# A hand-written list of 888 steps, put in another order: loads, matrix products and vector work of an RWKV layer with a feed-forward stage

## The chip, the cores and the metric

The kernel runs on one core of a Trainium2 chip. The metric is the device time of one execution in microseconds (us). Five engines work at once, each through its own queue of instructions in order: PE (the matrix engine, with its weight loads shown apart as PEld), DVE (the vector engine), ACT (activations), POOL (GpSimd) and SP (it only issues transfers here). Semaphores tie the queues together.

## The reference

Two stages follow each other: an RWKV attention over 4 batches, 8 heads, 768 positions and 48 values a head, and a feed-forward stage on its 3072 rows of 384 values.

```python
    for t in range(S):
        kt, vt, rt = (k[:, :, t].copy(), v[:, :, t].copy(), r[:, :, t].copy())
        cur = np.einsum('bhd,bhe->bhde', u[None] * kt, vt)
        y[:, :, t] = np.einsum('bhd,bhde->bhe', rt, state + cur)
        state = w[None, :, :, None] * state + np.einsum('bhd,bhe->bhde', kt, vt)
...
    h = x @ w_in                      # 384 -> 2048
    g = np.maximum(0.01 * h, h)
    return (g @ w_out).astype(np.float32)   # 2048 -> 384
```

## The kernel before

The positions are cut into 24 tiles of 128 (n = 0 to 23, six to a batch); a state of 8 heads x 48 x 48 is carried from tile to tile within a batch. The feed-forward stage takes two tiles at a time (m = 0 to 11).

The whole program is a list of steps, `ORDER`. A loop at the end of the kernel goes through it, and each step adds one instruction, or one group of matmuls, to the queue of its engine. So the list alone sets the order on every engine; waits are worked out afterwards from what each step reads and writes. Buffers are rings (`RINGS`): 10 slots for k and r, 10 for v, 6 for the masked scores `at`, 3 for `gT`. A number behind `@` in a step's name is the PSUM bank it takes; the next step on that bank waits until the last reader has let it go.

The steps are named by a letter and their tile. Those that the text speaks of, with their lines in the profile of before:

- `k3`, `r3`, `v3` (L284, POOL): the load of a tile of k, r or v from DRAM, cast to bf16. `i0` to `i3` (L296): a quarter of w_in. `w0` to `w3` (L300): a quarter of w_out. `p1` (L306): u. `p9` (L348, POOL): the ramp from which mask and tables are made.
- `P` (L399, DVE): k and r times their tables. `T` (L421, PE): transposes for tiles 0 to 7, which ACT copies out (`C`, L432). From tile 8 on `X` (L410, SP) transposes by DMA.
- `A` (L481, PE): scores; `M` (L491, L502, L505, DVE): scores under the mask, into `at`. For tiles 6 and up `E`, `f`, `R` (L442, L447, L452, DVE) make a token's own weight, and `L` (L467, POOL) lays it on the diagonal of `at` before `M` runs.
- `K` (L535, L539, L544, PE): keys times values; `V` (L560, DVE): v scaled, for tiles 0 to 5; `B` and `W` (L570 or L573, and L578, DVE): the next state. `Y` (L609, L613, PE): outputs of a tile; `O` (L627, ACT): copied to `xT`.
- `G` (L642, PE): 12 matmuls of 128 columns, the first product of the feed-forward stage for one tile, used for tiles 0 and 1; `J` (L664, PE): 6 matmuls of 256 columns, the same for two tiles; `j` (L673, ACT): the leaky relu.
- `b` (L735, DVE) and `t` (L716, DVE): sums for a seven-product form of the second matrix product; `Z` (L766, PE): one of the seven, 8 matmuls of 192 columns; `z` (L777, L782 on ACT, L787, L792 on DVE): its result; `o` (SP): the store.
- `F` (L387, PE): a matmul on a tile of ones whose result is not used.

```python
    for name in ORDER.split():
        unit[0] = name
        steps[name[0]](*(int(x) for x in name[1:].split("@")[0].split(".") if x))
```

Of the kernel before, what the change touches and what calls it, by code (L numbers as in the profile page):

```python
# [11 lines left out]
B, H, S, D = 4, 8, 768, 48  # L12
L = 128
# [4 lines left out]
E = 64  # L18
# [25 lines left out]
f7 J1.5@0 R6 O5 R7 j1.1 K6@7 L6 A7@23 B6 j1.5 A6@45 J2.6@6 j1.4 L7 M6 J2.1@7 k10 J0.5@0 M7 j2.1 J2.4@1 k11 j0.5
b1.0 Y6@7 j2.4 r10 Y7@0 b0.0 J2.5@5 O7 v8 b0.1 O6 J2.7@4 j2.6 b1.1 r11 J2.3@7 j2.7 J2.0@6 j2.5 k13 t0 j2.3
J2.2@0 j2.0 Z0.0@7 b1.2 j2.2 P9 Z0.1@1 z0.0 t1 X9 Z1.0@0 b2.0 J3.1@2 b0.3 Z0.2 P8 Z1.1@3 z0.2 z1.0 t2 X8 z0.1
Z0.3@4 j3.1 J3.3@5 E9 E8 Z0.4 k18 P10 j3.3 f8 K7@6 z1.1 Z1.2 t3 X10 k12 J3.2@2 z1.2 B7 r12 Z1.3@5 f9 E10 r15
z0.4 Z0.5 W7 P11 J3.6@6 r18 f10 X11 z0.5 Z0.6 b1.3 v16 Z1.4 R8 j3.6 E11 J3.7@1 L8 R9 J3.5@6 z1.3 j3.7 R10 r14
J3.4@5 z0.6 z0.3 j3.2 P13 v12 K8@1 J3.0@7 f11 j3.4 B8 j3.5 L9 A8@45 z1.4 A9@12 M8 Z1.5 k15 Z2.0@6 M9 L10 Z1.6
Y8@4 r16 W8 z1.6 j3.0 z1.5 Y9@5 P12 O8 A10@01 R11 X12 A11@23 O9 Z3.0@7 E12 L11 E13 M10 J4.4@4 X13 J4.3@5 v13  # L50
j4.4 b3.0 J4.7@0 v18 M11 J4.2@1 v14 J4.0@4 b3.1 j4.2 K9@2 j4.3 k14 J4.5@3 P15 z2.0 j4.7 J4.6@1 b3.3 X15 v19 j4.5
B9 Z3.1@5 j4.6 v10 b2.1 Z2.1@0 z3.0 z3.1 b2.2 k16 Z3.2 W9 b2.3 J4.1@3 k17 z3.2 z2.1 f12 Z2.2 f13 j4.1 v11 b3.2
Z2.3@2 z2.2 R12 j4.0 r19 K12@1 Z2.4 B12 L12 Z2.5 z2.3 R13 A12@12 z2.5 L13 A13@34 M12 Z3.3@0 k19 Z3.4 z2.4 P14
Z3.5 k21 z3.4 X14 Z2.6 z3.3 v15 M13 Z4.0@2 r17 K10@1 K13@0 B10 Y12@3 Y13@4 k20 O12 W10 Y10@1 P16 O13 Y11@3 v22
O10 P18 J6.0@4 O11 P19 z2.6 r20 J5.7@1 E16 E14 J5.4@3 E15 r22 j5.7 E17 b4.2 J6.1@6 j5.4 v20 z3.5 J5.6@1 f15 j6.1
f16 r23 J5.5@3 f14 j5.6 b4.0 J5.1@5 z4.0 v21 j5.5 B13 J6.6@6 P17 j5.1 f17 J5.3@3 X17 j6.0 R14 J5.0@5 b4.1 L14
j5.3 R15 J5.2@4 X18 j5.0 E18 Z3.6 r21 j5.2 b4.3 J6.7@3 z3.6 E19 k22 j6.6 W13 J6.5@7 o0 j6.7 X16 L15 A14@01 j6.5
A15@34 M14 J6.4@5 J6.3@6 j6.4 f18 o1 M15 J6.2@7 o7 o4 K14@5 Z4.1@0 o6 P20 Z4.2 B14 z4.1 j6.2 K15@1 W14 Z4.3@3
j6.3 P21 z4.2 R18 Y14@4 X21 f19 Y15@5 L18 O14 R19 A18@67 O15 K16@4 z4.3 Z4.4 P22 J7.7@5 B15 X22 z4.4 J7.3@3 W15
K18@1 Z4.5 X19 B18 Z4.6 B16 R17 J7.6@1 j7.7 M18 L17 X20 J7.4@4 j7.6 J7.5@5 v17 b6.0 j7.4 J7.2@1 j7.3 b5.0 o2 k23  # L60
z4.6 J7.0@4 j7.5 b5.1 v23 j7.2 J7.1@6 z4.5 R16 j7.0 o8 A17@01 W16 o3 j7.1 A16@23 L16 M17 o5 A19@45 Z5.0@7 L19
Z5.1@6 M16 Z6.0@0 E20 Z6.1@1 z6.0 M19 z5.0 K19@2 Z5.2 b6.1 Y18@3 Y19@4 E21 O18 Y17@5 B19 O19 Y16@3 f21 b5.3
J9.3@2 O16 f20 z6.1 Z6.2 O17 b6.2 Z5.3@3 b5.2 j9.3 E22 J8.3@4 R20 J8.0@5 R21 j8.3 L20 P23 J8.1@2 j8.0 L21 J9.2@4
# [12 lines left out]
"""


# [87 lines left out]
def bass_rwkv5_eagle__then__act_leaky_relu_kernel(  # L166
# [16 lines left out]
    NQK, NTP, NVS, NAT, NT, NX, NG, NO, NRK, NV = RINGS  # L183
# [4 lines left out]
    r_sb, k_sb = rk_sb[:, :, 0, :], rk_sb[:, :, 1, :]  # L188
    v_sb = SB("v_sb", [128, NV, H * E])
# [80 lines left out]

    def load_one(which, n):
        b, c = divmod(n, NC)
        t0 = c * L
        src = {"k": k, "r": r, "v": v}[which][b].rearrange("h t d -> t h d")[t0:t0 + L, :, :]
        if which == "v":
            dst = v_sb[:, n % NV, :].rearrange("p (h e) -> p h e", e=E)[:, :, 0:D]
        else:
            dst = {"k": k_sb, "r": r_sb}[which][:, n % NRK, :].rearrange("p (h d) -> p h d", d=D)
        key = (which, n % (NV if which == "v" else NRK))
        if which == "v" and n in VHW:  # L280
            io = 6 + n
            add("sp", lambda: SP.dma_start(hd(out_sb[io][:, :]), src), W=[("o", io, 0), ("o", io, 1)], dma=f"v{n}")
        else:
            add("pool", lambda: G.dma_start(dst, src), W=[key], dma=f"{which}{n}")  # L284
# [585 lines left out]
```

## Time and profile before

| | us |
|---|---|
| three runs | 165.57, 164.47, 164.97 |
| median | 164.97 |
| the profiled execution | 165.07 |
| its span (first to last instruction) | 163.3 |
| PE busy | 154.8 (95%) |
| DVE busy | 130.5 (80%) |
| ACT busy | 88.2 (54%) |
| POOL busy | 88.1 (54%) |

What lies between the span and the execution's time, 1.8 us, is outside the instructions. The busy shares are means over the whole span; the text below reads them stage by stage. A row of a timeline gives the start, the duration, the engine, the line, the operation, its result and operands, how many neighbours were merged into it, and in brackets how long the engine had been idle before it and who ended that. Durations of matmuls overlap, so the distance between two starts is the better measure there.

### The profile page before, as it was taken

What the parts mean: (1) busy time and instruction counts of PE and PEld (TensorE: products, weight loads), DVE (VectorE), ACT (ScalarE), POOL (GpSimd) and SP (SyncE); (2) the same over time, 40 slices, a digit from 0 to 9 for tenths busy, and PEclk for the clock granted to TensorE, in tenths of its full rate; (3) what the DMA queues carried; (4) which work ended last, traced back from release to release, by engine and by line L of the source; (5) the groups of instructions that cost most, each with busy time, mean ns of one, the idle gap of its engine ahead of it and who ended that gap; (6) DMA issues with size and microseconds to landing.
All of it is one profiled execution on the core that took longest, in us unless ns stands there. A gap on an engine that the chain in (4) does not pass through costs nothing.

```text
span 163.3 us, 5367 instructions
## 1 busy us (share of the span) xinstructions
PE 154.8 (95%) x2299; PEld 137.6 (84%) x2299; DVE 130.5 (80%) x260; ACT 88.2 (54%) x194; POOL 88.1 (54%) x101
## 2 busy tenths in 40 slices
PE   5959999999999698999999999999999999999993
PEld 1737888888999587999898998989989999999992
DVE  2678978979989999999999999999867770561552
ACT  3486686979443334722795528359057454637120
POOL 7999999996079958999974229223032000000000
PEclk9999999999999999999999999999999999999999
DMA  6999999999999999999999999900261000005025
GB/s 105 137 167 167 154 174 163 186 204 144 145 121 161 100 151 152 130 145 87 150 131 211 264 128 151 230 4 0 62 199 52 0 4 0 0 18 180 4 98 193
DMA packets 100234, 19.89 MB, mean 122 GB/s; under 512 B 93169, under 2 KB 100210, under 8 KB 100210
## 3 DMA queue, kind: packets, MB, share of 16 engines
q0 software_dynamic: 75616, 10.03, 93.8%
q1 hardware_dynamic: 23266, 9.12, 30.4%
q10 hardware_dynamic: 1328, 0.39, 1.0%
q8 instruction: 18, 0.29, 0.7%
q14 instruction: 6, 0.05, 0.1%
HBM read 20.65 MB, written 4.72 MB: 155 GB/s over the span
## 4 chain that ended last, share of the span: by engine, by line
PE 60%; POOL 21%; DVE 9%; DMA 6%; issue 2%; POOLq 0%; DVEq 0%
PE ps_all L766 28%; PE ps_all L664 25%; POOL rk_sb L284 11%; DMA rk_sb<-in_r_dram 6%; POOL v_sb L284 4%; PE ps_all L609 3%; PE ps_all L481 2%; POOL w_out_sb L300 2%; POOL w_in_sb L296 2%; DVE qk L399 2%; DVE at L505 2%; POOL at L467 1%; PE ps_all L539 1%; DVE out_sb L787 1%; DVE s_tok L452 1%
## 5 line engine op out<-in xcount | busy, mean ns | idle before, releaser
L673 ACT ACTIVATE gT<-ps_all 128x512 bf16<-128x512 f32 x92 | 52.0, 604 | 29.3 <-PE ps_all L766 14.1
L664 PE MATMUL ps_all<-xT,w_in_sb 128*128 128x256 bf16 x552 | 66.6, 273 | 0.5 <-DVE at L505 0.5
L664 PEld LDWEIGHTS ps_all<-xT,w_in_sb 128*128 128x128 bf16 x552 | 52.4, 98 | 7.3 <-DVE at L505 0.8
L467 POOL TENSOR_SCALAR_AFFINE_SELECT at<-s_tok 128x1024 bf16<-128x1024 f32 x18 | 20.6, 1155 | 27.0 <-DVE s_tok L452 26.9
L766 PE MATMUL ps_all<-tw,gs 128*128 128x192 bf16 x288 | 28.3, 246 | 0.1
L735 DVE TENSOR_TENSOR gs<-gT 128x1024 bf16<-128x1024 bf16 x24 | 16.1, 686 | 11.1 <-ACT gT L673 5.8
L284 POOL DMA_DIRECT2D rk_sb<-in_k_dram x23 | 21.0, 918 | 7.2 <-DVE ku L442 6.4
L766 PEld LDWEIGHTS ps_all<-tw,gs 128*128 128x128 bf16 x288 | 24.0, 98 | 0.4 <-issue 0.3
L505 DVE CAST_PREDICATED at<-mask,ps_all 128x1024 bf16<-128x1024 uint16 x18 | 21.5, 1216 | 2.0 <-PE ps_all L481 1.8
L284 POOL DMA_DIRECT2D v_sb<-in_v_dram x23 | 21.1, 923 | 0.6 <-PE ps_all L539 0.6
L284 POOL DMA_DIRECT2D rk_sb<-in_r_dram x23 | 21.3, 932 | 0.0
L766 PE MATMUL ps_all<-w_out_sb,gT 128*128 128x192 bf16 x192 | 19.8, 246 | 0.0
L787 DVE TENSOR_TENSOR out_sb<-ps_all,snap 128x192 f32<-128x192 f32 x37 | 12.6, 351 | 5.9 <-PE ps_all L766 5.8
L627 ACT ACTIVATE xT<-ps_all 128x384 bf16<-128x384 f32 x24 | 11.0, 494 | 11.5 <-PE ps_all L609 10.3
L777 ACT ACTIVATE snap<-ps_all 128x192 f32<-128x192 f32 x36 | 11.1, 338 | 11.3 <-PE ps_all L766 10.3
L766 PEld LDWEIGHTS ps_all<-w_out_sb,gT 128*128 128x128 bf16 x192 | 16.1, 98 | 0.5
L399 DVE TENSOR_TENSOR qk<-rk_sb,tab 128x768 bf16<-128x768 bf16 x23 | 13.9, 611 | 2.9 <-DMA rk_sb<-in_r_dram 2.7
L609 PE MATMUL ps_all<-at,v_sb 128*32 128x128 bf16 x384 | 10.4, 220 | 1.1 <-DVE vs L560 1.1
L432 ACT ACTIVATE tp<-ps_all 128x512 bf16<-128x512 f32 x16 | 9.0, 596 | 3.9 <-PE ps_all L421 3.6
L609 PEld LDWEIGHTS ps_all<-at,v_sb 128*32 128x32 bf16 x384 | 8.0, 96 | 3.1 <-DVE vs L560 1.4
L766 PE MATMUL ps_all<-w_out_sb,gs 128*128 128x192 bf16 x96 | 9.9, 246 | 0.0
L782 ACT ACTIVATE out_sb<-ps_all 128x192 f32<-128x192 f32 x11 | 3.7, 332 | 11.3 <-PE ps_all L766 11.3
(69 smaller groups left out, 196.6 us busy)
## 6 DMA issues: line engine op xcount, KB each, us to landing
out_dram<-out_sb SPq DMA_DIRECT2D x22, 192.0 KB, 2.8
rk_sb<-in_k_dram POOLq DMA_DIRECT2D x23, 96.0 KB, 6.0
rk_sb<-in_r_dram POOLq DMA_DIRECT2D x23, 96.0 KB, 6.0
v_sb<-in_v_dram POOLq DMA_DIRECT2D x23, 96.0 KB, 5.5
w_in_sb<-in_moe_w_in_dram POOLq DMA_DIRECT2D x4, 384.0 KB, 6.4
w_out_sb<-in_moe_w_out_dram POOLq DMA_DIRECT2D x4, 384.0 KB, 11.1
tp<-qk SPq DMA_TRANSPOSE x16, 5.2
out_sb<-in_k_dram ACTq DMA_DIRECT2D x1, 192.0 KB, 2.8
```

What stands on the lines that cost most here:

```text
L284: add("pool", lambda: G.dma_start(dst, src), W=[key], dma=f"{which}{n}")
L399: add("dve", lambda: V.tensor_tensor(qk[iq][:, :, 0:D], both, by, ALU.mult), R=[("r", n % NRK), ("k", n % NRK), "qtab", "ktab", ("qk0", iq ...
L467: add("pool", lambda: G.affine_select(out=at[ia][:, :, :, :].rearrange("p two m i -> p (two m) i"), in_=s_tok[i2][:, :].unsqueeze(2).to_br ...
L505: add("dve", lambda: V.copy_predicated(dst, mask[:, :].bitcast(mybir.dt.uint16).unsqueeze(1).to_broadcast([128, H, 128]), raw), R=keys + [ ...
L609: last = PE.matmul(ps_y[32 * q:32 * q + 32, 128 * s:128 * s + 128], a, m, start=first_mm and (s == 0 or whole), stop=last_mm and whole)
L627: add("act", lambda: A.activation(xT[m % NX][:, :, 128 * half:128 * half + 128], ps[i][:, 0:HD].rearrange("p (s t) -> p s t", t=128), AF.C ...
L664: last = PE.matmul(ps[i][:, 256 * f:256 * f + 256], w_in_sb[:, s, 128 * fb:128 * fb + 128], xT[ix][:, s, :], start=s == 0, stop=s == NSL - 1)
L673: add("act", lambda: A.activation(gT[ig][:, 2 * j:2 * j + 2, :].rearrange("p f t -> p (f t)"), ps[i][:, :], AF.Prelu, alpha=0.01), R=[key] ...
L735: add(eng, lambda: on.tensor_tensor(x[i][:, :, :], a, b, op), R=keys, W=[("gs", m % 2, i)])
L766: done = PE.matmul(ps[i][:, 0:NH], lhs[:, s, :], rhs[:, s, :], start=bool(opens) and s == 0, stop=s == HF - 1, skip_group_check=not (opens ...
L777: add("act", lambda: A.activation(snap[i2][j][:, :], ps[i][:, 0:NH], AF.Copy), R=[key], W=[("snap", i2, j)])
L787: add("dve", lambda: V.tensor_tensor(out_sb[io][:, cols], ps[i][:, 0:NH], snap[i2][j][:, :], ALU.add), R=[key, ("snap", i2, j), *after], W ...
```

## The change

The list is put in another order. No step of the computation is added or taken away; only the unused matmuls `F` become 10 where they were 21. The load function is written so that it could take two tiles at once, but the set that would ask for it, `PAIRED`, is empty, so each load has the same shape as before.

```diff
 VHW = {0}
+PAIRED = set()
...
 ORDER = """
-p3 p0 q1 k1 p10 p2 p8 p11 p4 F1.256.10@0 F1.256.2@1 k2 p5 p21@7 p6 p9 r1 p7 p15 p17 p13 p16 F1.512.18@6 v0 r2
...
+p3 p0 p9 q1 q0 p2 p8 p19 k3 p18 p14 p15 p13 p11 p4 p17 p10 p5 p16 r1 p21@0 p6 k1 p7 v0 p22 k2 p24 p23 r3 P0.1
...
     def load_one(which, n):
         b, c = divmod(n, NC)
-        t0 = c * L
-        src = {"k": k, "r": r, "v": v}[which][b].rearrange("h t d -> t h d")[t0:t0 + L, :, :]
...
+        m, slots = (2 if n in PAIRED else 1), (NV if which == "v" else NRK)
+        i = n % slots
+        src = {"k": k, "r": r, "v": v}[which][b].rearrange("h (c t) d -> t c h d", t=L)[:, c:c + m, :, :]
...
+        if m == 1:
+            src, dst = src[:, 0, :, :], dst[:, 0, :, :]
```

Three places matter for what follows. The lines of the new file stand one lower than those of the old one.

First POOL, from its first load on. Before, these are k1, k2, the ramp, r1, r2, the quarter i1 of w_in, r3, k3, v1, k5, r5, v2, i0:

```order
L284 DMA rk_sb<-in_k_dram 128x8x48 x2
L348 IOTA ramp 128x128
L284 DMA rk_sb<-in_r_dram 128x8x48 x2
L296 DMA w_in_sb<-in_moe_w_in_dram 128x3x512
L284 DMA rk_sb<-in_r_dram 128x8x48
L284 DMA rk_sb<-in_k_dram 128x8x48
L284 DMA v_sb<-in_v_dram 128x8x48
```

Now they are the ramp, k3, r1, k1 and k2, r3, v1, r2, and then i1:

```order
L347 IOTA ramp 128x128
L283 DMA rk_sb<-in_k_dram 128x8x48
L283 DMA rk_sb<-in_r_dram 128x8x48
L283 DMA rk_sb<-in_k_dram 128x8x48 x2
L283 DMA rk_sb<-in_r_dram 128x8x48
L283 DMA v_sb<-in_v_dram 128x8x48
L283 DMA rk_sb<-in_r_dram 128x8x48
L295 DMA w_in_sb<-in_moe_w_in_dram 128x3x512
```

The ramp and three loads of tiles 1 and 3 moved ahead of r2 and of the w_in quarter; after thirteen loads (k5, r5, v2, i0 and v3 follow in both) the same data have been asked for.

Second PE, at K3 (prod3, the matmuls on `wu`, and qk3) and the four G groups. Before: T5, then G1.1 and G1.0, K3, G0.0, and then Y2 begins (G0.1 stands ten steps earlier):

```order
L421 MATMUL ps_all<-ident,qk5 128x128 x8
L642 MATMUL ps_all<-xT0,w_in_sb 128x128 x24
L535 MATMUL ps_all<-wu,prod3 128x2 x4
L539 MATMUL ps_all<-v_sb,qk3 128x96 x4
L642 MATMUL ps_all<-xT0,w_in_sb 128x128 x12
L609 MATMUL ps_all<-at2,v_sb 32x128 x4
```

Now, from the last matmuls of Y2 (vs2) on:

```order
L612 MATMUL ps_all<-ident,vs2 128x128 x3
L641 MATMUL ps_all<-xT0,w_in_sb 128x128 x12
L534 MATMUL ps_all<-wu,prod3 128x2 x4
L538 MATMUL ps_all<-v_sb,qk3 128x96 x4
L641 MATMUL ps_all<-xT0,w_in_sb 128x128 x12
L608 MATMUL ps_all<-at3,v_sb 32x128 x4
```

K3 has moved behind Y2 and behind all G groups but the last.

Third DVE, around B8 (sum_t0), which frees the bank of A9 (before) or A8 (now), and M8 (at2). Before, P13 (qk1) and f11 (ku3) stand ahead of B8:

```order
L787 TENSOR_TENSOR out_sb0<-ps_all,snap0_0 128x192
L399 TENSOR_TENSOR qk1<-rk_sb,tab 128x16x48
L447 TENSOR_TENSOR ku3<-rk_sb,ku3 128x384
L573 TENSOR_TENSOR sum_t0<-ps_all,st2 128x384
L787 TENSOR_TENSOR out_sb3<-ps_all,snap1_1 128x192
L505 COPY_PREDICATED at2<-mask,ps_all 128x1024
```

Now:

```order
L398 TENSOR_TENSOR qk1<-rk_sb,tab 128x16x48
L451 TENSOR_REDUCE s_tok1<-ku1 128x8
L441 TENSOR_TENSOR ku3<-rk_sb,u_tab 128x384
L786 TENSOR_TENSOR out_sb2<-ps_all,snap1_0 128x192
L451 TENSOR_REDUCE s_tok0<-ku0 128x8
L451 TENSOR_REDUCE s_tok2<-ku2 128x8
L786 TENSOR_TENSOR out_sb0<-ps_all,snap0_0 128x192
L572 TENSOR_TENSOR sum_t0<-ps_all,st2 128x384
L446 TENSOR_TENSOR ku3<-rk_sb,ku3 128x384
```

P13 has moved ahead of three sums (R9, R8, R10), and f11 behind B8.

More of the change, by code (lines that the diff above doesn't have):

```diff
@@ L44 @@
[L44 to L63, printed above, removed]
@@ new lines @@
+f17 O14 R18 K16@7 O15 Z4.4 P22 L18 J7.3@3 R17 X22 z4.4 Z4.5 j7.3 L17 M18 J7.7@2 X19 v17 K18@3 Z4.6 W15 z4.5 z4.3
+J7.4@0 B16 o2 J7.5@1 b5.1 X20 j7.4 R19 J7.6@5 j7.7 b6.0 j7.5 L19 J7.0@0 j7.6 b6.2 o3 J7.1@6 z4.6 f16 j7.0 B18
+J7.2@7 j7.1 R16 A17@01 j7.2 W16 A19@23 L16 A16@45 M19 Z5.0@6 k23 Z6.0@7 z5.0 M16 Z6.1@2 r23 Z5.1@3 M17 K19@4
+Z5.2 b6.1 Y18@5 Y19@0 E22 O18 B19 Y16@1 O19 Y17@5 f22 E21 J9.3@4 R22 O17 O16 b5.2 J9.1@0 L22 j9.3 b6.3 J8.0@5
+z6.0 P23 Z5.3@1 j8.0 E20 X23 f21 J8.1@4 z5.2 W19 z5.1 z5.3 Z6.2 E23 j8.1 o8 J9.2@5 o6 f23 o7 b7.0 J8.3@1 j9.2 o9
@@ L283, in load_one @@
         else:
-            add("pool", lambda: G.dma_start(dst, src), W=[key], dma=f"{which}{n}")
+            add("pool", lambda: G.dma_start(dst, src), W=[(which, i + j) for j in range(m)], dma=f"{which}{n}")
     def v_cast(n):
```

62 lines of the change are left out of this document (36 added, 26 removed).

## Prediction

> **What bounds the kernel now.** I read the busy time by stage first, then who waited for whom, then the timelines of PE, DVE and POOL where PE stood still. The columns of the stages are the busy time (and count) of PE, PEld, DVE, ACT and POOL.
>
> ```profile
> 0.00:22.60 22.60, 18.86 (x304) 13.32 (x305) 15.69 (x43) 14.13 (x28) 21.42 (x30) 1.00 1.82 149
> 22.60:62.60 40.00, 38.09 (x570) 33.68 (x568) 37.31 (x69) 23.77 (x50) 31.45 (x36) 1.00 1.99 150
> 62.60:107.60 45.00, 44.98 (x738) 40.94 (x739) 44.21 (x85) 24.90 (x56) 30.67 (x33) 1.00 1.66 159
> 107.60:163.30 55.70, 52.91 (x691) 49.62 (x689) 33.34 (x66) 25.41 (x61) 4.59 (x4) 1.00 0.19 60
> ```
>
> From 22.60 us on PE is idle for 1.91 us in the second stage, 0.02 us in the third and 2.79 us in the last, nearly all of that after its last matmul. So PE sets the pace, and a new order can win in three ways only: the dense part begins earlier, the waits inside it go, or the tail shrinks. DVE is next: 44.21 of 45.00 us in the third stage, with no cover for more work there. The two waits that make up the 1.91 us are these:
>
> ```profile
> PE ps_all L481 <- DVE sum_t L573: 1.4, 1, 1.4
> PE ps_all L664 <- DVE at L505: 0.5, 1, 0.5
> ```
>
> The price of PE's work comes from the chain of waits, where the matmuls stand back to back (start, length, line and count):
>
> ```profile
> 75.68 0.34 PE ps_all L539 x8
> 77.53 7.32 PE ps_all L664 x66
> 148.75 11.89 PE ps_all L766 x144
> ```
>
> A J is 6 x 7.32/66 = 0.67 us, a Z 8 x 11.89/144 = 0.66 us, the usual K 0.17 us. Both lists hold the same J, Z, K, A and Y, so inside the dense part PE needs the same time in both.
>
> **The start.** The first J of before begins at 22.67 us; the set of PE steps that stands ahead of it is the same in the new list, but for the unused F. So the question is when the first J runs now.
>
> ```profile
> 3.61 0.23 DVE L357 TENSOR_SCALAR ident<-ramp 128x128 bf16<-128x128 f32 x1 [1.88 <-POOL ramp L348]
> 8.77 0.56 DVE L399 TENSOR_TENSOR qk<-rk_sb,tab 128x768 bf16<-128x768 bf16 x1 [2.15 <-DMA rk_sb<-in_r_dram]
> 12.04 0.95 POOL L284 DMA_DIRECT2D v_sb<-in_v_dram  x1
> v_sb<-in_v_dram POOLq DMA_DIRECT2D x1, 96.0 KB, 7.1
> 17.84 1.51 PE L642 MATMUL ps_all<-xT,w_in_sb 128*128 128x128 bf16 x24
> 19.29 0.24 PE L535 MATMUL ps_all<-wu,prod 128*128 128x2 bf16 x4
> 19.76 0.55 DVE L560 TENSOR_TENSOR vs<-v_sb,ps_all 128x384 bf16<-128x384 bf16 x1
> 22.67 2.13 PE L664 MATMUL ps_all<-xT,w_in_sb 128*128 128x256 bf16 x18
> ```
>
> The ramp, now first, ends DVE's 1.88 us of idling, but DVE waits next for the third load anyway (r1 before, at 8.77 us; k1 now, also third), so that gains nothing. The thirteenth load, v3, is the thirteenth in both lists: issued at 12.04, landed 7.1 us later at 19.1. K3 followed at 19.29 and V3 at 19.76, so neither the loads nor i1's later place (its G groups all start after 14.7 us, against about 13.4 for the eighth load) move this point. What does is PE's order. Before, K3 runs right after G1.1 and G1.0. Now it stands behind Y2 and G1.0, and Y2 behind V2. From the starts of PE's rows, a G group is 0.76 us (1.51 for two), and from G1.1 on the new list has G1.1, K2, G0.1, T5.1, Y2, G1.0, K3: 0.76 + 0.44 + 0.76 + 0.27 + 0.78 + 0.76 = 3.8 us from G1.1 to K3. G1.1 needs Y1, which I put at about 15.1 us by adding DVE's rows from P1 on, so G1.1 starts near 16.8, K3 near 20.6, V3 at 21.0, Y3 at 21.5 and the first J at 23.4. That is **0.7 us later**. The bounds: 0 if the G groups run while Y1 is awaited elsewhere, 1.5 if the chain slips by one T, C and D more.
>
> **The waits inside.** Here is what PE waited for, and the POOL rows beside it.
>
> ```profile
> L442 DVE TENSOR_TENSOR ku<-rk_sb,u_tab x18: 346/351/1242, 29.5 to 111.0; 128x384 bf16<-128x384 bf16 x18
> L447 DVE TENSOR_TENSOR ku<-rk_sb,ku x18: 345/351/1533, 30.9 to 112.3; 128x384 bf16<-128x384 bf16 x18
> 52.88 1.21 DVE L399 TENSOR_TENSOR qk<-rk_sb,tab 128x768 bf16<-128x768 bf16 x1
> 54.01 1.53 DVE L447 TENSOR_TENSOR ku<-rk_sb,ku 128x384 bf16<-128x384 bf16 x1
> 54.21 1.11 POOL L467 TENSOR_SCALAR_AFFINE_SELECT at<-s_tok 128x1024 bf16<-128x1024 f32 x1
> 55.47 0.54 DVE L573 TENSOR_TENSOR sum_t<-ps_all,st 128x384 bf16<-128x384 f32 x1
> 56.07 0.40 PE L481 MATMUL ps_all<-tp 48*128 48x128 bf16 x8 [1.39 <-DVE sum_t L573]
> 59.92 1.51 DVE L442 TENSOR_TENSOR ku<-rk_sb,u_tab 128x384 bf16<-128x384 bf16 x2
> 60.09 1.14 POOL L467 TENSOR_SCALAR_AFFINE_SELECT at<-s_tok 128x1024 bf16<-128x1024 f32 x1 [1.95 <-DVE s_tok L452]
> 62.62 1.59 PE L664 MATMUL ps_all<-xT,w_in_sb 128*128 128x256 bf16 x13 [0.55 <-DVE at L505]
> ```
>
> A step f has a median of 351 ns; f11 took 1533 and ended 0.2 us after the GpSimd select beside it; E13 likewise ended with the select of 60.09. So a two-input bf16 step on DVE that meets a select loses about 1 us, and B8, queued behind P13 and f11, came late; A9 waited 1.39 us for its bank. In the new list f11 stands behind B8, and between K8 and A8 PE has three more Z and J steps (2.0 us). Adding DVE's rows from P9 on (P9 cannot begin before k9, now the 26th small load):
>
> ```profile
> 30.20 1.02 POOL L284 DMA_DIRECT2D rk_sb<-in_k_dram  x1
> rk_sb<-in_k_dram POOLq DMA_DIRECT2D x1, 96.0 KB, 12.4
> ```
>
> The 26th of before (k8) was issued at 30.20 and landed 12.4 us later, at 42.6. From there DVE's steps to B8 sum to 10.3 us, with one wait of about 0.6 us for K7, which moved later on PE: B8 ends near 54.0, and A8 is due at 54.29 + 0.7 = 55.0. So the 1.39 us goes. M10, which set the 0.55 us, then ends near 60.6 and its J is due at 60.9: cover of only 0.3 us, gone if P12 meets the select L11. I keep half of that wait: the term is **-1.6 us** (bounds -1.94 and 0, the second if the lost time returns as in the row at 54.01). X9 to X11 and their transposes start 2 us later on SP, but A9 takes them ten microseconds afterwards.
>
> **A new wait late on.**
>
> ```profile
> 80.65 0.95 POOL L284 DMA_DIRECT2D rk_sb<-in_r_dram  x1
> 98.95 0.88 POOL L284 DMA_DIRECT2D rk_sb<-in_k_dram  x1
> rk_sb<-in_k_dram POOLq DMA_DIRECT2D x1, 96.0 KB, 5.3
> 100.79 2.19 POOL L467 TENSOR_SCALAR_AFFINE_SELECT at<-s_tok 128x1024 bf16<-128x1024 f32 x2
> 109.64 1.20 DVE L399 TENSOR_TENSOR qk<-rk_sb,tab 128x768 bf16<-128x768 bf16 x1
> ```
>
> r23 was issued at 80.65; now it is queued behind the select L16 and behind k23. L16 waits for R16, at about 101.4 on the old clock; with 1.1 for L16 and 0.9 for k23, r23 goes out at 103.4 and, at 5.3 us like k23, lands at 108.7, at worst at 110. Its reader P23 moves up to 108.6. Behind P23 on DVE stand E20, f21, W19 and z5.3, and J8.3 needs z5.3's bank at 111.3, 0.7 us after z5.3 is due. So P23 may lose 0 to 1.4 us, of which 0.7 is covered: 0 to 0.7 for PE; I take **+0.3**.
>
> The other moves cost nothing: r18 now waits for f8 where k18 waited for E8, both near 45.5 us; ACT is busy 24.90 of 45.00 us, and the stores at the end have the same last one.
>
> **The sum** is 0.7 - 1.6 + 0.3 = -0.6 us, from the profiled execution's 165.07: **164.4 us**, 0.3% under the median of 164.97. About 1% (163.3 to 166.6) is what a measurement of this kernel can tell from no change.
>
> **The rivals.** *All waits go and the start holds*: 165.07 - 1.94 = 163.1. For it: K3 may overlap more than I add; against it: PE's order at K3 in plain sight.
>
> *PE is cold for longer.*
>
> ```profile
> 3.77 2.95 PE L387 MATMUL ps_all<-ones 128*128 128x512 bf16 x13
> 7.80 0.58 PE L421 MATMUL ps_all<-ident,qk 128*128 128x128 bf16 x4
> 9.39 0.40 PE L421 MATMUL ps_all<-ident,qk 128*128 128x128 bf16 x4 [0.79 <-DVE qk L399]
> ```
>
> The same four transposes took 0.58 us at 7.80 and 0.40 at 9.39: PE came to full speed in between, about 6 us after its first matmul, and 13 F in a row filled the time from 3.77. Now 10 F are left, most of them behind steps that wait for data. If PE stays slow until the G groups, the short steps on the way (T, K, Y) cost 1.5 us more and half of the 3.8 us from G1.1 to K3 are spent again at half speed, 1.5: 164.4 + 3.0 = 167.4. Against it: from T1 on PE has work every few tenths of a microsecond in both lists. [...]
>
> *DVE is held by selects in the full stage*, the case on the other side.
>
> ```profile
> 84.25 0.78 DVE L442 TENSOR_TENSOR ku<-rk_sb,u_tab 128x384 bf16<-128x384 bf16 x1
> 85.55 1.24 DVE L442 TENSOR_TENSOR ku<-rk_sb,u_tab 128x384 bf16<-128x384 bf16 x1
> 86.72 1.24 DVE L578 TENSOR_TENSOR st<-sum_t,wl 128x384 bf16<-128x384 bf16 x1
> ```
>
> In the third stage of before three steps met a select and lost 0.43, 0.89 and 0.89 us, 2.2 in all. In the new list a sum R, which lets a select go, is followed at once by two-input steps in five places (R12 by b2.3; R14 by E15 and P19; R15 by b5.0, E18; R19 by b6.0, b6.2; R22 by b5.2, b6.3): 5 x 0.9 = 4.5 us, 2.3 more than before, on an engine with 0.79 us to spare in 45. If all meet, and J4.7's wait of 0.3 returns, the time is 164.4 + 2.3 + 0.3 = 167.0. It decides from the point where DVE's lead on PE, 0 to 1 us here, is used up. Against it: a step that starts before its select loses nothing, as the E of 346 ns, the median, show.
>
> **How the numbers follow.** Forecast 0.48 (its own range 163.4 to 165.7), all waits gone 0.24, cold PE 0.12, DVE held 0.16. Faster by over 1%: the second case and a rest of the first, 0.26; slower: most of the last two, 0.25; within: 0.49. The range goes from just under the second case, 162.7, to the price of the two slow ones, 167.2.
>
> **What would show it.** The first J after 23 us; no wait of PE for sum_t near 55 us; a wait of DVE for in_r_dram near 108 us; PE without idle time between. The forecast is wrong if PE waits over 1 us in any stage after 62 us, if the early transposes take 0.58 us beyond 12 us, or if the first J comes before 22.7.

## The result, and the profile after

The changed kernel takes 166.99 us (median of 6 runs, 166.85 to 167.61), the kernel before 165.27 us (6 runs). The ratio is 1.0111, with a 95% interval of 1.0068 to 1.0154: 1.1% slower, where 0.3% faster was forecast. The profiled execution has a span of 165.2 us, 1.9 us more than before. All ratios here leave out executions over 1.5% above the fastest of their kernel; only in `l10_later` are these many, five of twelve (the median of all twelve is 167.28 us).

First the same four stages as in the prediction (busy time and count of PE, PEld, DVE, ACT, POOL).

```profile
0.00:22.60 22.60, 16.33 (x263) 11.72 (x267) 15.62 (x42) 12.46 (x25) 21.63 (x30) 1.00 1.82 146
22.60:62.60 40.00, 38.60 (x604) 33.72 (x593) 35.58 (x68) 25.37 (x55) 29.75 (x34) 1.00 1.92 155
62.60:107.60 45.00, 44.28 (x683) 39.96 (x685) 43.74 (x82) 23.30 (x51) 31.96 (x34) 1.00 1.52 135
107.60:165.30 57.70, 54.80 (x772) 51.29 (x758) 35.06 (x71) 27.47 (x66) 7.85 (x5) 1.00 0.28 74
```

The first stage has 16.33 us of PE work where before had 18.86; of the 2.53 us between them 1.95 are unused matmuls (5.27 us before, 3.32 now). In the second PE is idle for 1.40 us, in the third for 0.72; before it was 1.91 and 0.02. So the start lost, and the waits inside were not removed but exchanged. What PE waited for, by line:

```profile
PE ps_all L420 <- DVE qk L398: 1.1, 1, 1.1
PE ps_all L608 <- DVE at L504: 0.8, 2, 0.5
PE ps_all L480 <- DVE st L569: 0.7, 1, 0.7
PE ps_all L663 <- issue: 0.6, 1, 0.6
PE ps_all L641 <- issue: 0.6, 1, 0.6
```

The waits for `sum_t` at A9 (1.39 us) and for `at` at J4.7 (0.55 us) are gone, the first as forecast, while the forecast had kept half of the second. New are two waits of Y8 and Y9 for M8 and M9, one of A19 for B18, and two that are put down to "issue": PE waited there for nothing that the profile shows. They stand in the middle of a group, behind the fifth matmul of G1.0 and behind the third of J1.5:

```profile
12.53 0.60 PE L420 MATMUL ps_all<-ident,qk 128*128 128x128 bf16 x4
19.81 0.44 PE L641 MATMUL ps_all<-xT,w_in_sb 128*128 128x128 bf16 x5
20.83 0.56 PE L641 MATMUL ps_all<-xT,w_in_sb 128*128 128x128 bf16 x7 [0.58 <-issue]
23.97 2.13 PE L663 MATMUL ps_all<-xT,w_in_sb 128*128 128x256 bf16 x18
35.63 1.80 PE L663 MATMUL ps_all<-xT,w_in_sb 128*128 128x256 bf16 x15 [0.58 <-issue]
```

The first row is T3.0 at 12.53 us, still 0.6 us long; in before the transposes were at 0.40 from 9.39 us on. The fourth row is the first J with its neighbours, at 23.97 us.

The two waits of Y8 and Y9 have one cause, which DVE's and POOL's timelines show together (W8 is L577, L10 the select at 56.64, M8 and M9 are L504):

```profile
55.72 0.92 POOL L283 DMA_DIRECT2D v_sb<-in_v_dram  x1
55.96 2.02 DVE L577 TENSOR_TENSOR st<-sum_t,wl 128x384 bf16<-128x384 bf16 x1
56.64 1.11 POOL L466 TENSOR_SCALAR_AFFINE_SELECT at<-s_tok 128x1024 bf16<-128x1024 f32 x1
58.16 2.34 DVE L504 CAST_PREDICATED at<-mask,ps_all 128x1024 bf16<-128x1024 uint16 x2
59.52 0.24 PE L608 MATMUL ps_all<-at,v_sb 128*32 128x128 bf16 x4 [0.35 <-DVE at L504]
60.56 0.24 PE L608 MATMUL ps_all<-at,v_sb 128*32 128x128 bf16 x4 [0.47 <-DVE at L504]
```

W8 took 2.02 us instead of 0.35 and ended 0.2 us after the select. The wait of A19 is the same story: one of two b (0.68 us alone) met the select L19, so B18 (L569) came late.

```profile
99.90 2.17 DVE L734 TENSOR_TENSOR gs<-gT 128x1024 bf16<-128x1024 bf16 x2
100.05 1.47 POOL L466 TENSOR_SCALAR_AFFINE_SELECT at<-s_tok 128x1024 bf16<-128x1024 f32 x1 [1.77 <-DVE s_tok L451]
102.26 0.54 DVE L569 TENSOR_TENSOR st<-ps_all,wl 128x384 bf16<-128x384 f32 x1
102.86 0.62 PE L480 MATMUL ps_all<-tp 48*128 48x128 bf16 x16 [0.72 <-DVE st L569]
```

### The profile page after: what moved, and what is told of

Its sections match the earlier page's. It is cut to its first block, busy times and chain, and to the rows that moved or that the text cites. A ratio compares the mean times of both kernels' runs of the same rounds, so it can differ in the third digit from the quotient of the medians.

```text
span 165.2 us, 5337 instructions
## 1 busy us (share of the span) xinstructions
PE 154.0 (93%) x2288; PEld 136.7 (83%) x2288; DVE 130.0 (79%) x260; ACT 88.6 (54%) x194; POOL 91.2 (55%) x101
## 4 chain that ended last, share of the span: by engine, by line
PE 84%; DVE 7%; DMA 3%; issue 2%; ACT 1%; POOL 1%; POOLq 0%
PE ps_all L663 34%; PE ps_all L765 32%; PE ps_all L608 6%; PE ps_all L480 4%; DMA rk_sb<-in_k_dram 3%; PE ps_all L420 2%; DVE at L504 2%; PE ps_all L538 2%; PE ps_all L641 2%; DVE gs L734 2%; POOL rk_sb L283 1%; ACT tp L431 1%; PE ps_all L386 1%; PE ps_all L612 1%; DVE qk L398 1%
## 5 line engine op out<-in xcount | busy, mean ns | idle before, releaser
L663 PE MATMUL ps_all<-xT,w_in_sb 128*128 128x256 bf16 x552 | 67.3, 273 | 0.6 <-issue 0.6
L466 POOL TENSOR_SCALAR_AFFINE_SELECT at<-s_tok 128x1024 bf16<-128x1024 f32 x18 | 23.7, 1340 | 23.2 <-DVE s_tok L451 20.0
L734 DVE TENSOR_TENSOR gs<-gT 128x1024 bf16<-128x1024 bf16 x24 | 17.7, 748 | 8.7 <-PE ps_all L663 4.0
L504 DVE CAST_PREDICATED at<-mask,ps_all 128x1024 bf16<-128x1024 uint16 x18 | 21.3, 1214 | 3.0 <-PE ps_all L480 2.0
L765 PE MATMUL ps_all<-w_out_sb,gT 128*128 128x192 bf16 x192 | 19.3, 246 | 0.0
L451 DVE TENSOR_REDUCE s_tok<-ku 128x8 f32<-128x384 bf16 x18 | 9.6, 541 | 0.0
```

What stands on the lines that cost most here:

```text
L466: add("pool", lambda: G.affine_select(out=at[ia][:, :, :, :].rearrange("p two m i -> p (two m) i"), in_=s_tok[i2][:, :].unsqueeze(2).to_br ...
L504: add("dve", lambda: V.copy_predicated(dst, mask[:, :].bitcast(mybir.dt.uint16).unsqueeze(1).to_broadcast([128, H, 128]), raw), R=keys + [ ...
L663: last = PE.matmul(ps[i][:, 256 * f:256 * f + 256], w_in_sb[:, s, 128 * fb:128 * fb + 128], xT[ix][:, s, :], start=s == 0, stop=s == NSL - 1)
L734: add(eng, lambda: on.tensor_tensor(x[i][:, :, :], a, b, op), R=keys, W=[("gs", m % 2, i)])
L765: done = PE.matmul(ps[i][:, 0:NH], lhs[:, s, :], rhs[:, s, :], start=bool(opens) and s == 0, stop=s == HF - 1, skip_group_check=not (opens ...
```

## Two theories, and how the experiments tell them apart

The account of the profile is: start +1.30 us (0.58 of it the first stop), old waits -1.94, new waits +1.54, second stop +0.58. That makes 1.48 of the 1.9 us; 0.16 more is the tail behind the last matmul (2.83 instead of 2.67 us), and 0.3 is spread over PE's rows. The theory has two parts. **Selects**: the change moved the meetings of selects with two-input steps, it did not remove them. **Borders**: PE stops where a new piece of its instructions begins. The page lists the packets that carry instructions (queue, packets, MB, share):

```profile
q8 instruction: 18, 0.29, 0.7%
```

18 packets of 0.29 MB are 16 KB each, and PE has 2 x 2288 matmuls and weight loads, 254 for each packet. Counted in the trace, the two stops come right behind PE's 449th and 961st instruction, 512 apart. That a packet holds 256 of PE's instructions is an estimate from these counts. The rivals: the start is late because PE was cold, because of the order of the loads, or because of the order of PE's and DVE's steps; the stops are a mark without a price.

### Two selects, one at a time

The select L10 moved behind the three loads v12, r16 and r14 (`l10_later`; the expectation counts four), and R19 with L19 behind b6.0, b6.2 and f16 (`r19_later`):

```diff
- W8 j3.0 A9@45 z1.4 L10 Z1.5 M8 Z2.0@7 v12 M9 Z1.6 r16 Y8@6 z1.5 Y9@1 b2.1 O8 r14 A10@23
+ W8 j3.0 A9@45 z1.4 Z1.5 M8 Z2.0@7 v12 M9 Z1.6 r16 Y8@6 z1.5 Y9@1 b2.1 O8 r14 L10 A10@23
```

```diff
- j7.4 R19 J7.6@5 j7.7 b6.0 j7.5 L19 J7.0@0 j7.6 b6.2 o3 J7.1@6 z4.6 f16 j7.0 B18
+ j7.4 J7.6@5 j7.7 b6.0 j7.5 J7.0@0 j7.6 b6.2 o3 J7.1@6 z4.6 f16 R19 L19 j7.0 B18
```

> The changed kernel with one GpSimd select, the one of tile 10, moved behind the four loads that follow it. Theory: the W of tile 8 took 2.02 us instead of 0.35 because it met this select; with the select gone from 56.6 us it takes under 0.5 us, the M of tiles 8 and 9 end about 1.5 us earlier, PE no longer waits 0.35 and 0.47 us for them, and the time falls by 0.8 to 1.1 us (about 166.0, 1.005 of before). Rival one: it was held by the load that GpSimd was issuing (55.72 to 56.64 us): W stays over 1 us, the waits stay, and the time stays at 167.0. Rival two: the select now meets the next steps of DVE and the wait returns at the M of tile 10: 167.0 as well, with W short.

> The changed kernel with the sum R of tile 19, and the select that it lets go, moved behind two steps b and one f on DVE. Theory: the second b took 0.89 us longer since it met this select, the B of tile 18 was late by as much, and PE waited 0.72 us for its bank at the scores of tile 19; now both b take 0.7 us, the wait goes, and the time falls by 0.6 to 0.9 us (about 166.2, 1.006 of before). Rival: DVE is short of time in this stage whatever the order; the select now holds another step (W of tile 16 or the next b), the wait reappears at the scores or outputs that follow, and the time stays within 0.3 us of 167.0.

`l10_later`: 1.0004 of before (0.9970 to 1.0039). W8 is short, Y8 and Y9 wait no longer, and the select now meets b2.1 (0.68 us alone), which brings back part of the wait at J4.7:

```profile
55.40 0.35 DVE L577 TENSOR_TENSOR st<-sum_t,wl 128x384 bf16<-128x384 bf16 x1
58.68 1.14 POOL L466 TENSOR_SCALAR_AFFINE_SELECT at<-s_tok 128x1024 bf16<-128x1024 f32 x1
58.95 1.43 DVE L734 TENSOR_TENSOR gs<-gs,gT 128x1024 bf16<-128x1024 bf16 x1
62.50 2.14 PE L663 MATMUL ps_all<-xT,w_in_sb 128*128 128x256 bf16 x18 [0.37 <-DVE at L504]
```

So the theory and its second rival each hold in part: 0.82 us of waits went, 0.37 came. Loads ran beside W8 here too (two, 55.16 to 56.97 us), and it took its 0.35 us.

`r19_later`: 1.0053 (1.0022 to 1.0084). The two b take 1.29 us together and A19 does not wait:

```profile
99.28 1.29 DVE L734 TENSOR_TENSOR gs<-gT 128x1024 bf16<-128x1024 bf16 x2
102.02 0.84 PE L480 MATMUL ps_all<-tp 48*128 48x128 bf16 x24
```

Both ratios were taken on a chip on which the changed kernel was measured in another set of runs (1.0115), and the executions of `l10_later` spread from 165.44 to 168.39 us, so what they say of the sums is rough; what the selects do is in the rows.

### The start, exchanged as a whole

> The changed kernel once more, as the measure for the three others on the same chip. Its work is dense from the first J on, so if the two stops for instructions (0.6 and 0.7 us) come and go between executions, the first J lies near 24 us with or without them (24.3 and 23.8 in the two runs that began with the same steps) and the time between 165.5 and 167.5 us, 1.003 to 1.011 of before. Rival: the stops are fixed to the list, so the profile shows both again at 20.8 and 35.6 us, and the ratio is again 1.011.

> The order of before up to its first J, and from there on the order of the change. Theory: the start (1.3 us) is the larger part of what the change costs and belongs to the steps ahead of the first J, so this kernel has its first J at 22.5 to 22.8 us and is 1.0 to 1.6 us faster than the changed kernel on the same chip, near the time of before (ratio 0.997 to 1.003): the waits of before at A9 and J4.7 are gone, but those of the change at Y8, Y9 and A19 stay. Rival: the start only moves the wait; the loads for tiles 8 to 11, in the order of the change, then hold DVE and PE in the stage after it, and the time stays at that of the changed kernel.

> The order of before up to its first J, the order of the change after it, and there the select of tile 10 behind the four loads and the sum R of tile 19 with its select behind b, b and f. Theory: first J at 22.6 us, no wait at A9 and J4.7 as in the change, none at Y8, Y9 and A19 as in the two earlier runs; a rest of 0.3 to 0.6 us of waits where the moved select meets the next b. 138 us of work from the first J make an end near 160.0: 1.2 to 2.0 us faster than before, ratio 0.988 to 0.993. Rival: each wait that goes lets the next step of DVE meet a select; the sum of the waits stays at 2 us, and the ratio at 0.997 to 1.003.

The changed kernel again: 1.0117 (1.0085 to 1.0148), with other stops in its profile (1.03 us at 21.62, 0.49 us at 29.74) and the first J at 24.77 us: the stops come and go, as the theory has it, but the time stays, as the rival has it. `old_start`, the steps of before up to the first J and then those of the change: 0.9983 (0.9954 to 1.0013). `mixed_best`, with both selects moved as well: 0.9930 (0.9907 to 0.9953). Since J1.2 took a bank too early in these two, they were built once more with one step changed, and with L10 behind one load instead of three:

```diff
- J1.2@7
+ J1.2@2
...
- z1.4 L10 Z1.5 M8 Z2.0@7 v12 M9
+ z1.4 Z1.5 M8 Z2.0@7 v12 L10 M9
```

> The order of before up to its first J and the order of the change from there on, as in old_start, but with J1.2 on another PSUM bank: in old_start and mixed_best J1.2 took the bank of the second transposes of tile 4 before they had been copied out, so these two computed tile 4 from wrong keys, with the same instructions. Theory: again at the time of before (ratio 0.995 to 1.002), so the start is worth 1.0 to 1.6 per cent, all that the change loses. Rival: what made old_start fast was the missing wait for that copy; with the bank free in time the ratio is over 1.005.

> As old_start2, with two moves of the change's order after the start: the select of tile 10 behind one load (v12) instead of ahead of it, and the sum R of tile 19 with its select behind b, b and f. Theory: the select of tile 10 now runs beside the steps M of tiles 8 and 9, which no select has stretched so far; so W of tile 8 takes 0.35 us, the next b 0.7, and neither Y8, Y9, J4.7 nor A19 waits: 0.3 us less than in mixed_best, ratio 0.989 to 0.993. Rival: M is held as the two-input steps are; Y8 or Y9 waits 0.5 us or more and the ratio is 0.995 or above.

> The other way about: the order of the change up to its first J, and the order of before from there on. Theory: the start costs 1.3 to 2.0 us whatever follows, and the waits of before (1.39 us at A9 and 0.55 us at J4.7) stay as they are set by DVE and GpSimd long after the start: ratio 1.008 to 1.013. Rival: the later start gives DVE and the loads time to catch up, the two waits shrink by what the start loses, and the ratio is 1.000 to 1.004.

`old_start2`: 0.9964 (0.9937 to 0.9992). `new_start`: 1.0174 (1.0112 to 1.0235). The two together place the loss in the part of the list up to the first J: with the start of before, the rest of the change gains 0.4%; with the start of the change, the rest of before is 1.7% slower. They exchange all of that part at once, its order, its loads and its unused matmuls. Nor is the first J of the profiles early each time: it is at 23.02 us in `old_start2` and 23.30 in `mixed2`, but at 24.26 in `old_start`, where K3 waited 1.17 us for v3 (that execution is the longest of its eleven). In the lists that begin as before, v3 was issued at 12.0 us and landed between 17.9 and 20.8. The waits of before stay whatever the start is, 1.19 us at A9 and 0.54 at J4.7 in `new_start`:

```profile
PE ps_all L479 <- DVE sum_t L571: 1.2, 1, 1.2
PE ps_all L662 <- ACT gT L650: 1.2, 1, 1.2
PE ps_all L662 <- DVE at L503: 0.5, 1, 0.5
```

The middle row is of the mixture itself: the first J of before takes the bank that the last G group of the change has just filled. So 1.7% is more than the start costs inside the change.

`mixed2` is the fastest kernel here: 0.9903 of before (0.9872 to 0.9934), 164.36 us against 165.86 on its chip. From 24 us to the last matmul PE waits nowhere for as much as 0.15 us:

```profile
24.00:62.60 38.60, 38.49 (x575) 34.15 (x574) 36.17 (x68) 23.87 (x51) 30.86 (x34) 1.00 1.95 157
62.60:107.60 45.00, 45.00 (x743) 41.08 (x741) 43.41 (x88) 25.13 (x55) 31.28 (x33) 1.00 1.52 134
```

The M beside the select L10 are not held (2.34 us for two, as in the change), but W8 still lost 0.89 us while two loads and no select ran on GpSimd:

```profile
54.18 1.79 POOL L285 DMA_DIRECT2D v_sb<-in_v_dram  x2
54.42 1.24 DVE L579 TENSOR_TENSOR st<-sum_t,wl 128x384 bf16<-128x384 bf16 x1
55.97 1.11 POOL L468 TENSOR_SCALAR_AFFINE_SELECT at<-s_tok 128x1024 bf16<-128x1024 f32 x1
```

In `l10_later` the same step beside the same loads took 0.35 us, with the select four loads away instead of two. How a select that is still to come can hold a step is open; the starts of GpSimd's rows are rough.

### What in the start it is: warmth, loads, order or borders

Before and after differ in the number of unused matmuls, 21 and 10. Two instructions each, so every later PE instruction stands 22 places earlier in the changed kernel. The first trial added 30 small ones (60 places) where PE waits; the second took 9 away from before, with the same number of columns.

```diff
- p21@0 p6 k1
+ p21@0 F19.32.40@6 p6 k1
...
- A0@01 q3 D0
+ A0@01 F11.32.41@4 q3 D0
```

> The changed kernel with 30 more unused matmuls of 32 columns, 19 and 11 of them, where PE waits for data anyway (3.8 to 5.6 us and 8.1 to 9.2 us). They move every later PE instruction 60 places on in its stream. Theory: the two stops of 0.58 us that the changed kernel's profile puts down to 'issue', 512 PE instructions apart, are PE waiting for its next 16 KB of instructions; after the shift the last 100 or so instructions before these borders take longer, so the stops shrink to under 0.2 us each: first J at 23.2 to 23.5 us instead of 23.97, and 1.0 to 1.3 us off the time (about 165.8 us, 1.004 of before). Rival: the two stops belong to the steps in which they fall (the fourth group of G, and J1.5), for a reason that the records do not name: they stay in the same steps, and the time stays within 0.3 us of 167.0.

```diff
- F1.128.8@5 ... F1.256.1@6 ... F1.128.28@0 ... F1.128.18@1 (and 11 more that were joined)
+ F1.512.31@6 (and 5 more of 512 columns)
```

> The kernel before with its unused columns in 12 matmuls instead of 21: the same 5632 columns, so the same PE time and the same warmth, but 18 PE instructions fewer ahead of everything else. Theory (PE waits for instructions at every 256th one when the instructions just before it run fast): the borders fall 18 instructions later in the work, where the run up to the second and third takes 2.1 and 1.7 us instead of 2.7 and 2.0; stops of 0.2 and 0.6 us appear at 26 to 27 us and at 33 to 34 us, put down to 'issue', and the time rises by 0.5 to 0.9 us (1.003 to 1.006 of before). Rival: the number of unused instructions does not matter: no stop in these places, ratio 1.000 within 0.002.

`fetch_after`: 0.9989 (0.9964 to 1.0015). The first stop did not shrink, it moved 60 instructions back in the work, from G1.0 into Y2; the one near 35 us is gone. The first J is at 24.11 us, not at the 23.2 to 23.5 of the expectation.

```profile
20.07 0.23 PE L609 MATMUL ps_all<-tp,st 128*32 128x128 bf16 x2 [0.58 <-issue]
```

`fetch_before`: 1.0010 (0.9980 to 1.0040) and no stop at either place; here the rival held. The borders alone make no stop: the instructions of this list stand only 4 places later than in the change, and it shows none.

Then warmth, and the chain to Y0:

```diff
- p21@0 p6 k1
+ p21@0 F4.512.40@6 p6 k1
...
- A0@01 q3 D0
+ A0@01 F2.512.41@4 q3 D0
```

```diff
- K0@0 C1.1 P3
+ K0@0 V0 C1.1 P3
...
- A1@12 i0
+ A1@12 Y0@7 O0 i0
...
- T3.1@2 C2.0 r4 O0 Y1@4
+ T3.1@2 G0.1@4 C2.0 r4 Y1@7
```

> The changed kernel with 6 more unused matmuls of 512 columns, 4 in PE's gap before the first transposes (3.8 to 5.6 us) and 2 in its gap before T1.0 (8.1 to 9.2 us). Theory: the start is late since the transposes, K and A ahead of 13 us run at 0.6 instead of 0.4 us a group; with these gaps closed PE is at full speed by 9.5 us, T1.0 and T1.1 take 0.4 us, the first J comes 0.5 to 1.0 us earlier (23.0 to 23.5), and the time falls by as much. Rival: the start is set by the loads and by the order of PE's groups (the 0.7 us of the prediction); the transposes get faster, but the first J stays at 23.8 to 24.3 us.

> The changed kernel with the chain to the first outputs pulled forward as in before: V0 on DVE right behind the scores of tile 0, Y0 on PE behind A1, its copy behind it on ACT, and G0.1 ahead of Y1, where PE waited 0.51 us. Theory: G0.1 and A2 (1.0 us of PE's time), which before had done by 16.4 us and the change not, are what the start loses; with G0.1 done early the first J comes 0.5 to 0.8 us sooner and the ratio is 1.005 to 1.008. Rival: PE is at 0.6 us a group until 13 us and waits for its instructions at 20.8 us whatever the order, so what is won is waited for again there: ratio 1.009 to 1.013.

`warm_start`: 1.0072 (1.0042 to 1.0102), 0.4% under the changed kernel on its chip. T1.0 takes 0.40 us, but the first J is at 24.03 us: PE stopped at the border for 0.66 us and went on at 20.50 us (0.58 and 20.83 in the change). `y0_early`: 1.0084 (1.0052 to 1.0117), 0.3% under the mean of the changed kernel; the intervals overlap, and its first J is at 24.04 us. Neither theory is borne out by that; in both, the first J stays where the rival of `warm_start` had it.

The last six, four on one chip:

```diff
- k3 ... r1 ... k1 ... k2 ... r3 ... v1 ... r2 ... i1
+ k1 ... k2 ... r1 ... r2 ... i1 ... r3 ... k3 ... v1
```

> The changed kernel as the measure for the three others on this chip: 1.009 to 1.014 of before.

> The same kernel as fetch_after (30 unused matmuls of 32 columns where PE waits), now beside the changed kernel on one chip. If the stops for instructions are a part of the loss, it is 0.6 to 1.3 us faster than the changed kernel, 1.002 to 1.007 of before, with no stop at 28 to 36 us. Rival: these stops only stand where another wait would stand, and it is within 0.3 us of the changed kernel.

> The changed kernel with GpSimd's loads 2 to 9 in the order of before (k1, k2, r1, r2, the w_in quarter, r3, k3, v1) and all other engines as in the change. If the order of the loads made the start late, the first J comes 0.5 us or more sooner and the ratio falls to 1.007 or below. Rival, which the landings favour (the w_in quarter landed at 13.6 us and is first used at 17, v3 landed no later than in before): no gain, or a loss, since T3.0 and P3, early in the order of the change, now wait for k3 (landed at 12.5 to 13.0 us in the order of before): ratio 1.010 to 1.018.

> The changed kernel with 26 more unused matmuls of 128 columns in PE's two gaps (16 from 3.8 us, 10 from 8.1 us): full speed from 9 us on, and every later instruction 52 places on. If (b) and (c) add up, this gives the gain of warm_start (0.7 us) and that of shift_again together: 1.000 to 1.004 of before, and the first J at 23.0 to 23.6 us. Rival: both remove the same stop and their gains do not add: 1.005 to 1.008, as warm_start.

`after_third`: 1.0115 (1.0058 to 1.0172). `shift_again`: 1.0015 (0.9987 to 1.0043), so the 30 small matmuls win 1.0% against the changed kernel beside it. `order_of_loads`: 1.0149 (1.0090 to 1.0207): the old order of loads wins nothing when the other engines keep the new order. DVE waits 1.52 us for k3, and PE is slow for longer (eight transposes still take 1.06 us at 16.57), so this does not price the loads alone:

```profile
13.02 0.56 DVE L398 TENSOR_TENSOR qk<-rk_sb,tab 128x768 bf16<-128x768 bf16 x1 [1.52 <-DMA rk_sb<-in_k_dram]
```

`warm_shift`, with 16 and 10 matmuls of 128 columns in the same two gaps: 1.0057 (1.0028 to 1.0086). The gains do not add; PE stops at the first border for 1.30 us, the longest of all. What is left is warmth against position:

```diff
- F1.512.17@7 ... F1.512.3@7 ... F1.512.6@1 ... F1.128.13@7 ... F1.128.26@4
+ F4.512.40@6 (behind p21) ... F1.512.41@4 (behind A0)
```

```diff
+ F4.32.40@6 (behind p21) ... F2.32.41@4 (behind A0)
```

> The changed kernel with five of its ten unused matmuls (between T1.0 and K1, 9.6 to 13.2 us) moved to PE's two gaps ahead of T1.0, all with 512 columns: as many PE instructions as in the change at every border, but PE at full speed from 9.5 us on. Warmth theory: 0.5 to 0.9 us faster than the changed kernel, 1.005 to 1.009. Rival, the borders: PE comes to the 449th instruction earlier and waits there the longer; no gain, 1.010 to 1.013.

> The changed kernel with 6 unused matmuls of 32 columns in PE's two gaps: every later PE instruction 12 places on, as in warm_start, but PE no warmer. If the borders are what counts, this has the gain of warm_start: 1.005 to 1.009. Rival, the warmth: no gain, 1.010 to 1.013.

`warm_moved`: 1.0110 (1.0068 to 1.0152). T1.0 and T1.1 take 0.62 us together, but PE did not stay warm: T3.0 takes 0.61 us at 12.29, and the trace's clock record has half the clock from 10.96 to 17.79 us. So this list was slow until later than the change, where the full clock begins at 13.00 us, and it is no test of warmth. PE stops for 1.15 us at 30.07:

```profile
9.82 0.62 PE L420 MATMUL ps_all<-ident,qk 128*128 128x128 bf16 x8 [1.60 <-DVE qk L398]
12.29 0.61 PE L420 MATMUL ps_all<-ident,qk 128*128 128x128 bf16 x4
30.07 2.12 PE L663 MATMUL ps_all<-xT,w_in_sb 128*128 128x256 bf16 x18 [1.15 <-issue]
```

`shift_12`: 1.0052 (1.0022 to 1.0083), with the full clock from 12.75 us, nearly as late as in the change, and one stop, ahead of the first J:

```profile
21.11 0.22 PE L613 MATMUL ps_all<-ident,vs 128*128 128x128 bf16 x1 [1.03 <-issue]
```

Two pairs speak against warmth. `warm_start` and `shift_12` have the same places, the first with the full clock from 6.87 us, and it is not the faster one (1.0072 and 1.0052, on two chips). `warm_shift`, with the full clock from 6.95 us, is slower than `shift_again`, which has it from 14.96 us only (1.0057 and 1.0015, on one chip). Of the four, tried one at a time, only the place of the instructions made the changed kernel faster by more than the error. The stops by place, from PE's timelines (a dash is under 0.15 us); the time that such a packet's transfer began, and when PE went on, are from the trace's packets:

```
kernel           places   stop behind PE's instruction ratio to
                 moved    449     705     961          before
the change       0        0.58    -       0.58         1.0111
after_again      0        1.03    0.49    -            1.0117
after_third      0        -       -       -            1.0115
warm_moved       0        -       1.15    -            1.0110
new_start        0        0.36    0.41    -            1.0174
fetch_before     +4       -       -       -            1.0010
shift_12         +12      1.03    -       -            1.0052
warm_start       +12      0.66    -       -            1.0072
warm_shift       +52      1.30    -       -            1.0057
fetch_after      +60      0.58    -       -            0.9989
shift_again      +60      -       -       -            1.0015
old_start2       +22      0.42    -       -            0.9964
before           +22      -       -       -            1

the change:  packet from 18.30, PE on at 20.83 (2.53 us later)
             packet from 33.36, PE on at 35.63 (2.27 us later)
warm_moved:  packet from 27.74, PE on at 30.07 (2.33 us later)
shift_12:    packet from 18.67, PE on at 21.11 (2.44 us later)
```

Shown is this. A few tiny matmuls in PE's gaps make the changed kernel faster: 12 places win 0.4 to 0.6% (`shift_12` lies under the 1.0110 to 1.0117 of the lists that were not moved; its interval just overlaps with that of `warm_moved` beside it), 60 places 1.0%. Where PE stops at one of the first three borders, it goes on 2.2 to 2.6 us after the packet's transfer began; in all twenty profiles none of the 340 first instructions behind a border began less than 2.2 us after it (the least is 2.22 us in before and 2.27 in the change). `r19_later` has one more stop of 0.29 us, behind the 1729th instruction, which is a border too.

Not shown is that the borders make the whole difference. The stops at the second and third border stand only in lists that were not moved (the one of 0.41 us in `new_start` the profile puts down to a copy of ACT), but `after_third`, `l10_later`, `r19_later`, `y0_early` and `order_of_loads`, unmoved too, have none at these places, and each profile is of one execution. `fetch_before` loses nothing with 4 places. And the gain does not show at the start: in the profiles of the five moved lists the first J is at 24.03 to 25.02 us, against 23.97, 24.77 and 24.12 in the change. What is shorter there is PE's idle time behind the first J, 1.11 to 1.24 us against 2.12, 1.65 and 1.69; a part of that is A19, which waits 0.30 us or less instead of 0.72, 0.30 and 0.67. What is left of the start's loss is not settled either: `y0_early` points to the order of PE and DVE, within its error.

## Why the prediction was wrong, point by point

The sum was -0.6 us, and the span grew by 1.9. Of the 2.5 us between them, 1.2 stand at the waits inside, 0.6 at the start and 0.6 at a second stop that had no term; r23 came out 0.3 better, and 0.4 is the tail and the spread over PE's rows.

**The start, +0.7.** The sign was right, the size and the reason were not. The profile has +1.30, other executions of the same steps +1.1 to +2.1. K3's place does not matter: from 16.24 to 23.97 us PE has no gap but the stop of 0.58. It has more left to do at 16 us, since G0.1 and A2 (1.0 us) came later, and it stops. The step that failed is the sentence "the set of PE steps that stands ahead of it is the same in the new list, but for the unused F": it puts at nothing, without a reason, that PE can stop behind its 449th instruction. The stop there took 0.58 us in this profile, 1.03 in the second and nothing in the third. What makes the rest of the delay stays open: `y0_early`, which does G0.1 early, has its first J at 24.04 us all the same.

**The waits inside, -1.6.** The two waits went in every profile of the change (-1.94 us). The step that failed is taking credit for that without the other side of the same meetings: L10 met W8 (+0.82 at Y8 and Y9) and L19 met b6.2 (+0.72, +0.30 and +0.67 in the three profiles), so -0.40 us was left of the -1.6. `l10_later` and `r19_later` show it: with the select moved, W8 takes 0.35 us and the waits at Y8 and Y9 go, and the two b take 1.29 us and the wait at A19 goes. I looked at where the selects had stood and did not follow them to where they stand now; only in the third stage did I price that, as a rival. `old_start2` has what the change is worth inside: 0.4%, half of what the terms inside, -1.6 and +0.3, gave.

**r23, +0.3.** No wait. r23 was issued at 105.34 us and P23 began without idling before it:

```profile
105.34 0.88 POOL L283 DMA_DIRECT2D rk_sb<-in_r_dram  x1
110.38 0.54 DVE L398 TENSOR_TENSOR qk<-rk_sb,tab 128x768 bf16<-128x768 bf16 x1
```

**The rivals.** "All waits go" fell with the start. "DVE held by selects" had the right kind of loss: 0.82 us came in the second stage and 0.72 in the third, against its 2.3 in the third alone. It is the rival that came nearest, and it had 0.16; that its 167.0 us is the measured time is luck, since it takes the start at 0.7 us and has no stops, and the start and the second stop made 1.88 us. The argument against it, that a step that starts before its select loses nothing, did not hold: W8 began 0.68 us before the select's row and ended 0.2 us after it, as far as GpSimd's rows can be trusted. "PE is cold for longer" had its sign (T3.0 0.60 us at 12.53), but its condition, slow until the G groups at 17 us, was not met: four transposes take 0.39 us again at 13.46. Half speed, which its price takes, is in the traces: transposes in a row start 107 ns apart at 7.80 us in before and 56 ns apart at 9.45, and in the change 107 at 12.61 and 56 at 13.51. The price itself was wrong, as half of 3.8 us is 1.9 and not 1.5, and the two pairs above show no gain from warmth.

**The signs.** The first J after 23 us and the missing wait for `sum_t` came true, the wait for `in_r_dram` and the gapless PE did not. That the early transposes were slow beyond 12 us was named as what would make the forecast wrong; it was seen, and no run shows that it cost anything.

How a select holds a step no run shows, only how much is lost. W8 takes 0.35 us with the select away and 2.02 with it near: it lost 1.67 us near a select of 1.11, and 0.89 in `mixed2` with none beside it.

## What to carry to other kernels

Here moving a step off a collision moved the collision (A9 lost its wait of 1.39 us, Y8 and Y9 got 0.82): follow the instruction that collides to its new neighbours before taking credit for the wait that goes. Work that is "unused" still has a place in the instruction stream (6 unused matmuls, 12 places, won 0.4 to 0.6% here); when a list gets shorter ahead of dense short matmuls, look for stops put down to "issue" at equal distances of instructions (here 256 or a multiple), and try a few tiny instructions in an idle gap. And split a change by its stages (old start with new rest, and the reverse) before explaining any of it: two runs showed here that the part with the larger count of moves gained and the small one lost.

## What the runs showed of the hardware that I had not expected

18 packets of instructions, 16 KB each, are moved while the kernel runs, one for every 254 PE instructions on average. Stops of 0.29 to 1.30 us appear behind PE's 449th, 705th, 961st and, once, 1729th instruction, differently from one execution to the next: 0.58 us, 1.03 us and none behind the 449th in three of the change. None of the 340 first instructions behind a border began less than 2.2 us after its packet's transfer did. 6 unused matmuls of 32 columns won about 0.6%. PE fell back to half its clock at 10.96 us in `warm_moved`, after idling for 1.60 us up to 9.82, and had it until 17.79 (0.979 on average over the execution). A two-input bf16 step on DVE lost 1.67 us near one select of 1.11 us; M, a predicated copy, lost nothing beside a select in `mixed2` (2.34 us for two, as in the change, where none ran beside them).
